# Decays by row transfers, outputs of two steps in token rows, and a new order for all engines

## The chip, the cores and the metric

The kernel runs on one core of a Trainium2 chip. Its engines work side by side, each on its own list of instructions: TensorE (PE, matrix products, with PEld its weight loads), ScalarE (ACT), VectorE (DVE), GpSimd (POOL) and SyncE (SP, which only issues transfers here). Transfers (DMA) are issued by SP, ACT and POOL and carried out by 16 DMA engines. The time is that of one execution on the device, in microseconds (us), as the median of some runs.

## The reference

Two layers, one behind the other. The first is a gated linear attention over 4 batches, 8 heads, 768 tokens and a head size of 48:

```python
f = 1.0 / (1.0 + np.exp(-f_logit))
for t in range(S):
    state = f[:, :, t, :, None] * state + np.einsum('bhd,bhe->bhde', k[:, :, t], v[:, :, t])
    y[:, :, t] = np.einsum('bhd,bhde->bhe', q[:, :, t], state)
```

Its output, as 3072 tokens of 384 values, goes through a gated feed-forward layer with 1536 hidden columns:

```python
gate = np.maximum(x @ w_gate, 0.0)
val = x @ w_val
return (gate * val @ w_out).astype(np.float32)
```

## The kernel before

The 768 tokens are cut into 6 chunks of 128 for each of 4 batches, 24 pieces in all. They are worked off in six steps (c = 0 to 5) of four positions (b = 0 to 3). The eight pieces of steps 0 and 1 are taken as four *units* of two chunks of one batch (function `place`); from step 2 on the step is the chunk and the position is the batch.

An operation is named by letters, step and position (`hq02` is `hq` of step 0, position 2). For one piece:

- `L` load q, k, v and the logits f (`load`, L408 and L413); `ef`, `ln` make -log f (ACT, L484 and L487, for two positions at once).
- `cum` sums the logs over tokens on PE (L505 and L509, later L514). In steps 2 to 4 it also sums each head's columns over the whole chunk, as four matmuls of one column (L517); `dc` makes of these the decay of the state (ACT, L545; L538 in units).
- `ek`, `eq` are the two exponentials (ACT, L528 and L530) into `expo`, `hk`, `hq` the scaled k and q, `hats` (POOL L552 or DVE L553); `v` copies v.
- In steps 0 and 1, `tk`, `tq` transpose them on PE (L564) and `ck`, `cq` copy the result to `qkT`; later `xh` does it by a transposing transfer that SP issues (L572).
- `s` makes the scores (L596, L662), `m` masks them (DVE), `y` (and `yi` in units) multiplies them with v and q with the state, `kv` the update of the state (L784, L707), `ss`, `sd` (L458, L460) the new state with the decay `dec`.
- The output goes to `xT`, with the hidden index on partitions. In steps 0 to 3 (mark `t` of `X_WAY`) `y` is computed turned, as 28 narrow matmuls that write 32 partitions each (L757; L684 and L720 in units), and one copy `x` brings it to `xT`. In steps 4 and 5 (mark `x`), `y` has tokens on partitions, as 4 matmuls of 96 and 8 of 48 columns (L764, L768); `n` copies it to `xn`, and `xx`, a transposing transfer issued by SP (L628), turns it into `xT`.

For each step the feed-forward layer follows: for 12 hidden groups j a gate `g` and a value `u` (three matmuls of 512 tokens each, L804), a relu `r` (L809, L810), a product `p` (L812), then for each position the output `o` in three groups of four matmuls (L825), a copy `d` and a store `S` (L835). The first four hidden groups of step 0 are split into halves of two positions. The weights come as groups by POOL (`wg`, `wv`, `wo`, L435); `wv4+4` is hidden groups 4 to 7.

The order of each engine is written out by hand or by a planner outside of the program, as lists of numbers of operations (`ORDER`). A negative entry stands for filler matmuls on zeros. `BANKS` gives the bank of PSUM for every result in the order of PE. `Plan.link` derives who depends on whom from what is read and written, `lay_out` sets the order, and `waits` makes semaphore waits of it. `HELD` adds waits by hand, mostly for transfers. An engine takes its list strictly in order; so does SP with the transfers that it issues.

Of the kernel before, what the change touches and what calls it, by code (L numbers as in the profile page):

```python
# [6 lines left out]
ALU = mybir.AluOpType  # L7
# [4 lines left out]
NB, NE, NH, NQ, NM, NV, NA, NN, NS, NX, NG, NR, NO = 3, 3, 6, 6, 5, 6, 3, 4, 2, 2, 2, 4, 3  # L12
UNITS = 4
PE_HATS = set(range(0, 8))
X_WAY = "t" * 16 + "x" * 8
# [10 lines left out]
        45, ~60100, 74, 85, ~3512, 82, ~3512, 90, 80, 92, 121, ~1512, 95, 110, 101, 126, ~4512, 116, ~2512, 100, 128,  # L26
# [216 lines left out]
def bass_hgrn2_outer__then__ffn_reglu_kernel(  # L243
# [29 lines left out]
    expo = sb("expo", [128, NE, 2, HD], F32)  # L273
# [681 lines left out]
```

## Time and profile before

| | us |
|---|---|
| median of 3 runs | 193.43 (192.94 to 194.12) |
| the profiled execution | 193.01 |
| its span, first to last instruction | 191.3 |
| PE busy | 180.6 |
| DVE busy | 137.4 |
| ACT busy | 92.0 |
| POOL busy | 59.2 |

The page gives the busy time of each engine, the span in 40 slices (one digit is the busy share in tenths), the transfers, the chain of work that ended last, and the costliest groups of instructions. A row of such a group reads: line, engine, operation, output and inputs, shapes, count, busy time, mean of one in ns, idle time before them and who ended it. A timeline row begins with start and duration in us; its duration is that of the whole row, and matmuls overlap, so that the time that one takes of PE is the distance to the next start.

### The profile page before, as it was taken

What the parts mean: (1) busy time and instruction counts of PE and PEld (TensorE: products, weight loads), DVE (VectorE), ACT (ScalarE), POOL (GpSimd) and SP (SyncE); (2) the same over time, 40 slices, a digit from 0 to 9 for tenths busy, and PEclk for the clock granted to TensorE, in tenths of its full rate; (3) what the DMA queues carried; (4) which work ended last, traced back from release to release, by engine and by line L of the source; (5) the groups of instructions that cost most, each with busy time, mean ns of one, the idle gap of its engine ahead of it and who ended that gap; (6) DMA issues with size and microseconds to landing.
All of it is one profiled execution on the core that took longest, in us unless ns stands there. A gap on an engine that the chain in (4) does not pass through costs nothing.

```text
span 191.3 us, 4793 instructions
## 1 busy us (share of the span) xinstructions
PE 180.6 (94%) x1977; PEld 108.4 (57%) x1996; DVE 137.4 (72%) x249; ACT 92.0 (48%) x200; POOL 59.2 (31%) x88
## 2 busy tenths in 40 slices
PE   7597999989899999999999999999999999999994
PEld 7364785455655556655555654556656554455562
DVE  4299877986758778669868779988688485655620
ACT  3969663264477546497654574372233132301112
POOL 5638531741036702047371610492600000000000
PEclk9999999999999999999999999999999999999999
DMA  6999999969999999989999999999763300000223
GB/s 163 318 296 216 159 209 264 161 123 251 225 221 206 240 201 246 235 191 200 197 182 215 245 175 175 243 251 178 98 151 108 99 4 0 3 0 0 109 98 126
DMA packets 110278, 32.43 MB, mean 170 GB/s; under 512 B 103472, under 2 KB 110000, under 8 KB 110256
## 3 DMA queue, kind: packets, MB, share of 16 engines
q1 hardware_dynamic: 88960, 25.04, 61.7%
q0 software_dynamic: 3744, 3.54, 12.2%
q10 hardware_dynamic: 17552, 3.54, 10.0%
q8 instruction: 16, 0.26, 0.6%
q14 instruction: 6, 0.05, 0.1%
HBM read 25.95 MB, written 4.72 MB: 160 GB/s over the span
## 4 chain that ended last, share of the span: by engine, by line
PE 85%; DVE 8%; DMA 3%; issue 2%; ACT 0%; DVEq 0%; ACTq 0%
PE ps L804 46%; PE ps L825 25%; DVE hats L553 4%; DMA q_in<-in_q_dram 3%; PE ps L596 2%; PE ps L757 2%; PE ps L564 2%; PE ps L514 1%; DVE gT L812 1%; PE ps L662 1%; PE ps L684 1%; PE ps L784 1%; DVE ptm L669 1%; PE ps L768 1%; PE ps L764 1%
## 5 line engine op out<-in xcount | busy, mean ns | idle before, releaser
L812 DVE TENSOR_TENSOR gT<-relu,ps 128x512 bf16<-128x512 bf16 (+1 forms) x76 | 47.7, 653 | 19.7 <-PE ps L804 17.5
L804 PE MATMUL ps<-xT,wv 128*128 128x512 bf16 (+1 forms) x220 | 53.6, 367 | 0.6 <-issue 0.2
L804 PE MATMUL ps<-xT,wg 128*128 128x512 bf16 (+1 forms) x219 | 52.6, 368 | 0.6
L825 PE MATMUL ps<-wo,gT 128*128 128x384 bf16 (+2 forms) x300 | 52.0, 320 | 0.0
L809 ACT ACTIVATE relu<-ps 128x512 bf16<-128x512 f32 (+1 forms) x42 | 23.9, 576 | 47.8 <-PE ps L804 24.2
L825 PEld LDWEIGHTS ps<-wo,gT 128*128 128x128 bf16 x300 | 27.7, 98 | 18.3
L804 PEld LDWEIGHTS ps<-xT,wg 128*128 128x128 bf16 x228 | 23.6, 108 | 20.5 <-issue 0.4
L804 PEld LDWEIGHTS ps<-xT,wv 128*128 128x128 bf16 x228 | 23.3, 108 | 18.3
L552 POOL TENSOR_TENSOR hats<-q_in,expo 128x384 bf16<-128x384 f32 x17 | 17.9, 1058 | 30.2 <-DMA q_in<-in_q_dram 12.2
L810 DVE TENSOR_SCALAR relu<-ps 128x512 bf16<-128x512 f32 (+1 forms) x34 | 21.7, 654 | 5.4 <-PE ps L804 5.3
L552 POOL TENSOR_TENSOR hats<-k_in,expo 128x384 bf16<-128x384 f32 x17 | 17.7, 1050 | 21.2 <-ACT expo L528 14.9
L604 DVE TENSOR_TENSOR ptm<-ps,tri 128x512 bf16<-128x512 f32 x32 | 20.5, 684 | 5.1 <-PE ps L596 5.1
L831 ACT ACTIVATE osb<-ps 128x384 f32<-128x384 f32 (+1 forms) x16 | 7.6, 484 | 25.0 <-PE ps L825 22.2
L528 ACT ACTIVATE expo<-ps 128x384 f32<-128x384 f32 x24 | 11.7, 496 | 6.1 <-DVE hats L553 2.6
L530 ACT ACTIVATE expo<-ps 128x384 f32<-128x384 f32 x24 | 11.8, 492 | 2.0 <-PE ps L517 1.9
L460 POOL TENSOR_TENSOR st<-ssum,dec 128x384 bf16<-128x384 f32 x10 | 8.6, 864 | 10.0 <-DVE ssum L458 10.0
L669 DVE TENSOR_TENSOR ptm<-ps,tmask 128x512 bf16<-128x512 f32 x16 | 10.0, 678 | 2.1 <-PE ps L662 2.1
L484 ACT ACTIVATE f_in<-f_in 128x768 f32<-128x768 f32 x12 | 10.1, 840 | 2.8 <-DMA f_in<-in_f_logit_dram 2.8
L458 DVE TENSOR_TENSOR ssum<-ps,st 128x384 f32<-128x384 f32 x16 | 8.8, 550 | 2.7 <-PE ps L784 2.5
L553 DVE TENSOR_TENSOR hats<-q_in,expo 128x384 bf16<-128x384 f32 x7 | 8.2, 1167 | 3.4 <-DMA q_in<-in_q_dram 3.4
L487 ACT ACTIVATE bneg<-f_in 128x768 bf16<-128x768 f32 x12 | 10.1, 841 | 1.0 <-ACT osb L831 0.8
L564 PE MATMUL ps<-ident,hats 128*128 128x128 bf16 x64 | 5.5, 220 | 4.0 <-DVE hats L553 3.0
(78 smaller groups left out, 159.2 us busy)
## 6 DMA issues: line engine op xcount, KB each, us to landing
v_in<-in_v_dram SPq DMA_DIRECT2D x12, 384.0 KB, 5.5
out_dram<-osb SPq DMA_DIRECT2D x23, 192.0 KB, 2.3
k_in<-in_k_dram SPq DMA_DIRECT2D x10, 384.0 KB, 7.1
q_in<-in_q_dram SPq DMA_DIRECT2D x9, 384.0 KB, 5.8
f_in<-in_f_logit_dram SPq DMA_DIRECT2D x8, 384.0 KB, 4.8
f_in<-in_f_logit_dram ACTq DMA_DIRECT2D x4, 384.0 KB, 6.6
q_in<-in_q_dram ACTq DMA_DIRECT2D x3, 384.0 KB, 5.6
wv<-in_moe_w_val_dram POOLq DMA_DIRECT2D x2, 384.0 KB, 6.7
```

Source lines behind the costliest of these rows:

```text
L484: add(f"ef{c}{b0}", by("ACT", lambda: sc.activation(raw, raw, AF.Exp, scale=-1.0), act_(n)), keys, keys, key=P)
L528: add(f"ek{c}{b}", by("ACT", lambda: sc.activation(ex[:, 1, :], bc.ap[:, 0:HD], AF.Exp, scale=1.0), act_(HD)), [bc], [f"expk{ei}"], key=P + 1)
L530: add(f"eq{c}{b}", by("ACT", lambda: sc.activation(ex[:, 0, :], bc.ap[:, 0:HD], AF.Exp, scale=-1.0), act_(HD)), [bc], [f"expq{ei}"], key=P ...
L552: return {**by("POOL", lambda: gp.tensor_tensor(o, i_, e_, ALU.mult), pool_(HD)), **by("DVE", lambda: ve.tensor_tensor(o, i_, e_, ALU.mult ...
L553: **by("DVE", lambda: ve.tensor_tensor(o, i_, e_, ALU.mult), dve_(HD))}
L604: add(f"m{c}{b}{j}", by("DVE", lambda b=b, j=j, mi=mi: ve.tensor_tensor(ptm[mi][:, j, :, :], s[b, j].ap[:, :].rearrange("p (n t) -> p n t" ...
L669: add(f"m{c}{b2[i]}{j}", by("DVE", lambda i=i, j=j, mask=mask: ve.tensor_tensor(ptm[mi[i]][:, j, :, :], s[j, i].ap[:, :].rearrange("p (n t ...
L804: z = te.matmul(bank.ap[:, 0:n], wt[:, kt, w_cols(j)], xT[xi][:, kt, n0:n1], start=(kt == 0), stop=(kt == NK - 1))
L809: add(f"r{c}{b0}.{j}", {**by("ACT", lambda: sc.activation(rdst, gate.ap[:, 0:n], AF.Relu), act_(n)), **by("DVE", lambda: ve.tensor_scalar_ ...
L810: **by("DVE", lambda: ve.tensor_scalar_max(rdst, gate.ap[:, 0:n], 0.0), dve_(n))}, [gate], [f"relu{ri}"], key=P)
L812: add(f"p{c}{b0}.{j}", by("DVE", lambda: ve.tensor_tensor(gT[gi][:, j, n0:n1], rdst, val.ap[:, 0:n], ALU.mult), dve_(n)), [val, f"relu{ri} ...
L825: z = te.matmul(o.ap[:, 0:e1 - e0], gT[gi][:, j, b * C:(b + 1) * C], wo[:, j, e0:e1], start=(j == 0), stop=(j == NJ - 1))
```

## The change

Four things change.

**Decays as rows.** For the pieces 8 to 19 (steps 2 to 4) the four one-column matmuls in `cum` and `dc` are gone. The last row of `expq`, the exponential at the chunk's last token, holds the same factors. For each pair of positions `xd` fetches it with two small transfers, one for the even and one for the odd heads, from one partition to 48 partitions with 32 bytes each. For that `expo` becomes `expk` (two buffers in place of three) and `expq` (two buffers for pairs, with the head size as the slowest index, so that neighbours in it lie 64 bytes apart). `dec` is laid out anew. A new `eq` into a buffer waits for the `xd` that read it.

**Outputs in token rows.** Steps 2 and 3 get the mark `x` too.

**Smaller constants.** `zeros` has 128 columns, a filler reads them four times; `tlow` shares space with `ssum`. `FOLD`, new in `place` and `load`, has the value of `UNITS`, so that it changes nothing here.

**New orders.** All lists of `ORDER`, `BANKS` and `HELD` are new.

```diff
-NB, NE, NH, NQ, NM, NV, NA, NN, NS, NX, NG, NR, NO = 3, 3, 6, 6, 5, 6, 3, 4, 2, 2, 2, 4, 3
+NB, NE, NH, NQ, NM, NV, NA, NN, NS, NX, NG, NR, NO = 3, 2, 6, 6, 5, 6, 3, 4, 2, 2, 2, 4, 3
+FOLD = 4
+ROW_DECAYS = set(range(8, 20))
+NEQ = 2
-X_WAY = "t" * 16 + "x" * 8
+X_WAY = "t" * 8 + "x" * 16
...
-    expo = sb("expo", [128, NE, 2, HD], F32)
+    expk, expq = sb("expk", [128, NE, HD], F32), sb("expq", [128, NEQ, D, 2, 2, NP], F32)
...
-    decs = sb("dec", [128, NA, B, NP, 2], F32)
+    decs = sb("dec", [128, NA, 2, B, NP], F32)
...
-    tlow = [sb(f"tlow{i}", [128, C], BF16) for i in range(2)]
+    tlow = [ssum[NS - 1][:, C // 2 * i:C // 2 * (i + 1)].bitcast(BF16) for i in range(2)]
-    zeros = sb("zeros", [128, 512], BF16)
+    zeros = sb("zeros", [128, 128], BF16)
...
+        rows = w in ROW_DECAYS
...
             x = te.matmul(bc.ap[:, 0:HD], tri[:, :], bn[:, :, 0:D])
-            if c < NC - 1:
+            if ch < NC - 1 and not rows:
                 for p in range(NP):
                     x = te.matmul(bc.ap[:, HD + p:HD + p + 1], bn[:, 2 * p:2 * p + 2, :].rearrange("p h d -> p (h d)"), ones[:, :])
...
-        ex = expo[:, ei, :, :]
+        ex = (expq[:, eqi, :, :, b % 2, :].rearrange("q d j p -> q p j d"),
+              expk[:, ei, :].rearrange("q (p j d) -> q p j d", p=NP, j=2))
...
+        elif rows and b % 2:
+            b0, c0 = place(c, b - 1)
+            def decay_rows(eng):
+                for j in range(2):
+                    at, to = expq[C - 1:C, eqi, 0, j, 0, 0:1], decs[64 * j:64 * j + D, ai, j, b0, 0:1]
+                    x = eng.dma_start(bass.AP(tensor=to.tensor, offset=to.offset, ap=[list(to.ap[0]), [1, 2 * NP]]),
+                                      bass.AP(tensor=at.tensor, offset=at.offset, ap=[list(at.ap[0]), [4 * NP, D], [1, 2 * NP]]))
+                    if j == 0:
+                        x.then_inc(xd.sem, 16)
+                return x
+            xd = add(f"xd{c}{b - 1}", {**by("SP", lambda: decay_rows(sy), (0.8, 0.8)), **by("ACT", lambda: decay_rows(sc), (0.8, 0.8))},
+                     [f"expq{eqi}_0", f"expq{eqi}_1", f"dec{ai}"], [f"dec{ai}_{b0}", f"dec{ai}_{bt}"], key=P + 2)
+        elif rows:
+            pass
...
         def scaled(src, xh, xe):
-            o, e_ = hats[:, hi, xh, :, 0:D], ex[:, xe, :].rearrange("p (h d) -> p h d", h=H)
-            i_ = src[:, b % 2, :, :]
+            o, e_ = hats[:, hi, xh, :, 0:D].rearrange("q (p j) d -> q p j d", p=NP), ex[xe]
+            i_ = src[:, b % 2, :, :].rearrange("q (p j) d -> q p j d", p=NP)
```

The orders, with the names in place of the numbers, at the places that matter below (F is a filler: count and columns):

```
PE before:   cum00 cum01 [3 F512] tq00 [3 F512] tk01 tk00 tq01 cum03 [F512] s00 cum02 kv00 tk03 [4 F512] tk02 [2 F512] y00 tq03 tq02
             yi01 kv02 s02 g00.3 cum12 g00.2 cum10 u00.3 u00.2 g00.1 y02 yi03 ...
PE after:    cum01 cum00 [2 F512] cum03 cum02 tk01 [2 F512] tk00 [2 F512] tq01 tq00 [F512] tk02 s00 kv00 [2 F512] tq02 [2 F512] tq03 tk03
             y00 yi01 s02 cum10 g00.3 cum12 g00.2 kv02 cum11 y02 yi03 u00.1 ... g00.4 g00.5 tk11 tk10 cum13 ...
ACT after:   ef00 ln00 ef02 ln02 ek01 ek00 eq01 dc00 ek03 eq02 eq00 ek02 ck00 eq03 v01 dc02 ck02 Lq1.0 Lq1.2 ef12 cq02 ef10 ln10 x01
             ln12 eq10 v02 ek10 dc10 eq11 ... r00.6 ek12 eq13 ...
POOL after:  ... hk00 hq01 hk02 v00 hq02 hq03 mtri wv0+2 wg0+2 wv2+2 sd10 v03 wv4+4 wg4+4 hq11 ... hk11 ...
SP before:   Lf0.0 Lf0.2 Lk0.0 Lv0.0 Lk0.2 Lv0.2 Lq0.2 Lf1.2 Lf1.0 Lq1.2 Lq1.0 Lk1.0 Lk1.2 Lv1.2 Lv1.0 ...   (Lq0.0 from ACT)
SP after:    Lf0.0 Lf0.2 Lk0.0 Lq0.0 Lk0.2 Lv0.0 Lq0.2 Lf1.2 Lf1.0 Lv0.2 Lk1.0 Lk1.2 Lv1.0 ...   (Lf1.0 held for wg2+2, Lk1.0 for wv4+4)
PE after, end of step 2:  ... y23 o13.0 cum33 y21 cum30 o12.8 y20 o13.4 o11.0 cum32 kv23 o11.4 o13.8 cum40 o11.8 u20.1 g20.3 ...
PE after, end of step 3:  ... y30 o21.0 o21.4 cum42 y31 o21.8 o20.0 o20.4 o20.8 kv32 o22.8 o23.8 g30.1 ...
SP after, step 2:         ... xh21 xh20 Lf4.0 Lk3.0 S03 xx22 S01 xx23 xx21 xx20 S10 Lv3.0 ...
```

By engine, DVE takes 19 of the 48 `hk` and `hq` (14 before), 11 of the 16 `sd` that can go to either engine (6 before), and 29 of the 76 relus (34 before).

More of the change, by code (lines that the diff above doesn't have):

```diff
@@ L332, in select @@
         add("s" + name, by("POOL", lambda: gp.affine_select(out=ap, in_=ap, **kw), (0.24, 0.29)), [name], [name], key=key)
-    fill("DVE", "zeros", zeros[:], 0.0, 256, -30)
+    fill("DVE", "zeros", zeros[:], 0.0, 64, -30)
     fill("POOL", "tri", tri[:], 1.0, 128, -12 if UNITS else -20)
@@ L352, in bass_hgrn2_outer__then__ffn_reglu_kernel @@
                                                                            channel_multiplier=-2), (0.24, 0.29)), [f"tlow{i}a", f"tlow{i}b"], [f"tlow{i}"], key=-16)
-            add(f"al{i}", by("DVE", lambda low=low, i=i: ve.tensor_tensor(tmask[i][:], tmask[i][:], low[:], ALU.add), (0.12, 0.2)), [f"tlow{i}", f"tmask{i}"], [f"tmask{i}"], key=-15)
+            add(f"al{i}", by("DVE", lambda low=low, i=i: ve.tensor_tensor(tmask[i][:], tmask[i][:], low[:], ALU.add), (0.12, 0.2)), [f"tlow{i}", f"tmask{i}", f"ssum{NS - 1}"], [f"tmask{i}"], key=-15)
         fill("DVE", "pair", pair[:], 0.0, 2, -17)
@@ L398, in place @@
         u = 2 * g + pos // 2
-        return (u % B, u // B * 2 + pos % 2) if u < UNITS else (pos, g)
+        return (u % B, u // B * 2 + pos % 2) if u < FOLD else (pos, g)
     def load(item):
@@ L410, in load @@
             return dma(op, f"{n}{slot}_0", "SP", 64, 0.0193)
-        src = bass.AP(tensor=srcs[n].tensor, offset=b0 * H * S * D + c * C * D, ap=[[D, C], [S * D, (b1 - b0) * H], [1, D]])
-        dst = ld[n][:, slot_of(n, c, b0 // 2), b0 % 2:b0 % 2 + b1 - b0, :, 0:D].rearrange("p b h d -> p (b h) d")
+        dst = ld[n][:, slot_of(n, c, b0 // 2), b0 % 2:b0 % 2 + b1 - b0, :, 0:D]
+        bt, ch = place(c, b0)
+        if 2 * c + b0 // 2 < FOLD:
+            src = bass.AP(tensor=srcs[n].tensor, offset=bt * H * S * D + ch * C * D, ap=[[D, C], [C * D, b1 - b0], [S * D, H], [1, D]])
+        else:
+            src = bass.AP(tensor=srcs[n].tensor, offset=bt * H * S * D + ch * C * D, ap=[[D, C], [S * D, (b1 - b0) * H], [1, D]])
+            dst = dst.rearrange("p b h d -> p (b h) d")
         op = add("L" + item, {**by("SP", lambda: sy.dma_start(dst, src), (0.42, 0.42)), **by("ACT", lambda: sc.dma_start(dst, src), (0.5, 0.5))}, [], in_keys(n, c, b0, b1), key=c * 40 + b0 * 10 - 20 + 0.1 * len(slots))
@@ L450, in new_state @@
         t4 = lambda t: t[:, 0:HD].rearrange("p (n j e) -> p n j e", n=NP, j=2)
-        rate = dec[ai][:, b, :, :].unsqueeze(3).to_broadcast([128, NP, 2, D])
+        rate = dec[ai][:, :, b, :].rearrange("q j p -> q p j").unsqueeze(3).to_broadcast([128, NP, 2, D])
         dk = [f"dec{ai}_{b}", f"dec{ai}"]
@@ L470, in front @@
         w = c * B + b
-        two, cc, bt = w < 2 * UNITS, w // 2 // B * 2, w // 2 % B
+        two, (bt, ch) = w < 2 * UNITS, place(c, b)
+        cc = ch - b % 2
         P = w * 10
         bi, bj = (w // 2) % NB, w % 2
-        ei, hi, qi, ai = w % NE, w % NH, w % NQ, c % NA
+        ei, eqi, hi, qi, ai = w % NE, w // 2 % NEQ, w % NH, w % NQ, ch % NA
         fin, kin, qin, vins = (halves(n, slot_of(n, c, b // 2)) if two else ld[n][:, slot_of(n, c, b // 2), :, :, 0:D] for n in "fkqv")
@@ L523, in front @@
         else:
-            add(f"cum{c}{b}", pe(cum, mm(HD) + (mm(1) * 4 if c < NC - 1 else 0)), ["tri", "ones", f"bneg{bi}", f"bn{bi}_{bj}"], [bc],
+            add(f"cum{c}{b}", pe(cum, mm(HD) + (mm(1) * 4 if ch < NC - 1 and not rows else 0)), ["tri", "ones", f"bneg{bi}", f"bn{bi}_{bj}"], [bc],
                 key=P, opens=[bc])
-        ex = expo[:, ei, :, :]
-        add(f"ek{c}{b}", by("ACT", lambda: sc.activation(ex[:, 1, :], bc.ap[:, 0:HD], AF.Exp, scale=1.0), act_(HD)), [bc],
+        ex = (expq[:, eqi, :, :, b % 2, :].rearrange("q d j p -> q p j d"),
+              expk[:, ei, :].rearrange("q (p j d) -> q p j d", p=NP, j=2))
+        parts = lambda t: t.rearrange("q (p j d) -> q p j d", p=NP, j=2)
+        add(f"ek{c}{b}", by("ACT", lambda: sc.activation(ex[1], parts(bc.ap[:, 0:HD]), AF.Exp, scale=1.0), act_(HD)), [bc],
             [f"expk{ei}"], key=P + 1)
-        add(f"eq{c}{b}", by("ACT", lambda: sc.activation(ex[:, 0, :], bc.ap[:, 0:HD], AF.Exp, scale=-1.0), act_(HD)), [bc],
-            [f"expq{ei}"], key=P + 1)
+        add(f"eq{c}{b}", by("ACT", lambda: sc.activation(ex[0], parts(bc.ap[:, 0:HD]), AF.Exp, scale=-1.0), act_(HD)), [bc],
+            [f"expq{eqi}_{b % 2}"], key=P + 1)
         if two and bj == 0:
@@ L541, in front @@
             add(f"dc{c}{b}", by("ACT", decay2, (0.24, 0.35)), [bc, f"dec{a0}", f"dec{a0 + 1}"], [f"dec{a0}_{bt}", f"dec{a0 + 1}_{bt}"], key=P + 2)
-        elif c < NC - 1 and not two:
+        elif rows and b % 2:
+            b0, c0 = place(c, b - 1)
+            assert c0 == ch and bt == b0 + 1
+            def decay_rows(eng):
[8 more added lines that the diff above has]
+                     [f"expq{eqi}_0", f"expq{eqi}_1", f"dec{ai}"], [f"dec{ai}_{b0}", f"dec{ai}_{bt}"], key=P + 2)
+            dma(xd, f"dec{ai}_{b0}", "SP", 6, 0.013)
+            slots[f"dec{ai}_{b0}"][1] += 16
+            xd.goal += 16
+        elif rows:
+            pass
+        elif ch < NC - 1 and not two:
             def decay():
                 for j in range(2):
-                    x = sc.activation(dec[ai][64 * j:64 * j + 64, b, :, j], bc.ap[64 * j:64 * j + 64, HD:HD + NP], AF.Exp, scale=-1.0)
+                    x = sc.activation(dec[ai][64 * j:64 * j + 64, j, bt, :], bc.ap[64 * j:64 * j + 64, HD:HD + NP], AF.Exp, scale=-1.0)
                 return x
-            add(f"dc{c}{b}", by("ACT", decay, (0.23, 0.34)), [bc, f"dec{ai}"], [f"dec{ai}_{b}"], key=P + 2)
+            add(f"dc{c}{b}", by("ACT", decay, (0.23, 0.34)), [bc, f"dec{ai}"], [f"dec{ai}_{bt}"], key=P + 2)
         def scaled(src, xh, xe):
-            o, e_ = hats[:, hi, xh, :, 0:D], ex[:, xe, :].rearrange("p (h d) -> p h d", h=H)
-            i_ = src[:, b % 2, :, :]
+            o, e_ = hats[:, hi, xh, :, 0:D].rearrange("q (p j) d -> q p j d", p=NP), ex[xe]
+            i_ = src[:, b % 2, :, :].rearrange("q (p j) d -> q p j d", p=NP)
             return {**by("POOL", lambda: gp.tensor_tensor(o, i_, e_, ALU.mult), pool_(HD)),
@@ L554, in front @@
         add(f"hk{c}{b}", scaled(kin, 1, 1), in_k("k") + [f"expk{ei}", f"hats{hi}"], [hk_(hi)], key=P + 2)
-        add(f"hq{c}{b}", scaled(qin, 0, 0), in_k("q") + [f"expq{ei}", f"hats{hi}"], [hq_(hi)], key=P + 2)
+        add(f"hq{c}{b}", scaled(qin, 0, 0), in_k("q") + [f"expq{eqi}_{b % 2}", f"hats{hi}"], [hq_(hi)], key=P + 2)
         if w in PE_HATS:
@@ L736, in back @@
         P = w * 10
+        bt, ch = place(c, b)
         hi, qi, mi, vi, xi = w % NH, w % NQ, w % NM, w % NV, c % NX
@@ L739, in back @@
         y = Bank("a")
-        s_old = st[b][(c + 1) % 2]
-        s_key = [f"S{b}_{(c + 1) % 2}"] if c else []
+        s_old = st[bt][(ch + 1) % 2]
+        s_key = [f"S{bt}_{(ch + 1) % 2}"] if ch else []
         def tiled():
@@ L745, in tiled @@
             rounds = []
-            if c:
+            if ch:
                 for r in range(NK):
@@ L761, in natural @@
         def natural():
-            if c:
+            if ch:
                 for p in range(NP):
@@ L768, in natural @@
                 z = te.matmul(y.ap[:, h * D:(h + 1) * D], ptm[mi][:, h % 2, h // 2, :], vp[:, at:at + D],
-                              start=(c == 0 and h == 0), stop=True, skip_group_check=True)
+                              start=(ch == 0 and h == 0), stop=True, skip_group_check=True)
             return z
@@ L773, in back @@
         if X_WAY[w] == "t":
-            add(f"y{c}{b}", pe(tiled, (7 if c else 4) * mm(C), "c"), need + [f"vpad{vi}"], [y], key=P + 7, opens=[y])
+            add(f"y{c}{b}", pe(tiled, (7 if ch else 4) * mm(C), "c"), need + [f"vpad{vi}"], [y], key=P + 7, opens=[y])
             out_way(c, b, y)
         else:
-            add(f"y{c}{b}", pe(natural, (mm(96) * 4 if c else 0) + mm(D) * 8), need, [y], key=P + 7, opens=[y])
+            add(f"y{c}{b}", pe(natural, (mm(96) * 4 if ch else 0) + mm(D) * 8), need, [y], key=P + 7, opens=[y])
             out_way(c, b, y)
-        if c < NC - 1:
+        if ch < NC - 1:
             kv = Bank("a")
@@ L887, in run @@
                     eng.wait_ge(sems[d.eng], d.val)
+                n = fill % 1000
+                row = zeros[:, 0:n] if n <= 128 else zeros[:].unsqueeze(1).to_broadcast([128, n // 128, 128])
                 for _ in range(fill // 1000):
-                    te.matmul((op.opens[0].ap if op.opens else banks[7])[:, 0:fill % 1000], zeros[:, 0:128], zeros[:, 0:fill % 1000],
+                    te.matmul((op.opens[0].ap if op.opens else banks[7])[:, 0:n], zeros[:], row,
                               start=True, stop=True, skip_group_check=True)
```

8 lines of the change are left out of this document (4 added, 4 removed), and 104 rows, old and new, of tables (BANKS, ORDER).

## The prediction

> **What bounds the kernel now.** I read the page first (busy times, slices, chain), then the windows of ten microseconds, then the chain and the timeline at the places where the change works.
>
> ```profile
> span 191.3 us, 4793 instructions
> PE 180.6 (94%) x1977; PEld 108.4 (57%) x1996; DVE 137.4 (72%) x249; ACT 92.0 (48%) x200; POOL 59.2 (31%) x88
> DVE  4299877986758778669868779988688485655620
> DMA  6999999969999999989999999999763300000223
> PE 85%; DVE 8%; DMA 3%; issue 2%; ACT 0%; DVEq 0%; ACTq 0%
> ```
> ```profile
> 30.00:40.00 10.00, 9.78 (x55) 5.10 (x54) 9.96 (x13) 4.03 (x9) 5.71 (x7) 1.00 1.02 196
> 50.00:60.00 10.00, 9.40 (x228) 5.80 (x229) 6.78 (x13) 6.83 (x14) 3.30 (x4) 1.00 1.36 231
> 100.00:110.00 10.00, 10.00 (x166) 6.29 (x168) 7.78 (x14) 4.66 (x11) 4.28 (x6) 1.00 1.29 231
> ```
>
> TensorE bounds it: 94% busy, 85% of the chain. The window rows give, after span and length, the busy time of PE, PEld, DVE, ACT and POOL, then the clock and the DMA share. From 100 to 110 us PE has no gap, from 50 to 60 it lacks 0.6. So a matmul removed behind 53 us is worth its own time, and every new wait there is lost in full. The second resource is the DMA: its slices read 9 until about 130 us, and its share passes 1.
>
> **The sum, part by part.** The profiled execution took 193.01 us: 191.3 of span and 1.7 around it. The median of the three runs, 193.43, lies 0.4 above it. I sum against 193.01.
>
> *(a) Decays of steps 2 to 4 as rows.* It removes four one-column matmuls from each of twelve `cum`, and twelve pairs of small exponentials on ACT; it adds six pairs of small transfers, two pairs issued by SP and four by ACT.
>
> ```profile
> 79.28 0.08 PE ps L517 x4
> 79.36 0.67 PE ps L825 x4
> 80.03 1.68 PE ps L757 x112
> 81.71 0.76 PE ps L825 x4
> 82.70 0.36 PE ps L784 x8
> ```
> ```profile
> 92.67 0.24 PE L517 MATMUL ps<-ones,bneg 128*128 128x1 bf16 x4
> 92.77 0.32 PE L514 MATMUL ps<-bneg,tri 128*128 128x384 bf16 x1
> L545 ACT ACTIVATE dec<-ps 64x4 f32<-64x4 f32 x24 | 4.0, 166 | 1.1 <-PE ps L517 0.9
> ```
>
> Four such matmuls hold PE for 0.08 us in the chain and 0.10 from 92.67 to 92.77; I take 0.09. Twelve times 0.09 is **1.1 us**, all in stages where PE has no gap. The 4.0 us on ACT count as nothing: ACT is 48% busy. The transfers do not exist in before. Their reader is the state product `sd`, and the state is first read by `y` of the next step, some 30 us later (six steps in a span of 191.3), against landings of up to 7 us for loads a hundred times as large (rows under c). That distance hides them. Without it, SP and ACT would each hold behind the issue, and a late landing would hold the `eq` two pairs later, which now waits for the transfer to have read its buffer. Bounds: nothing, and one landing of 7 us on ACT, which PE would feel only in part; I take nothing, since `eq` stands a whole step behind.
>
> *(b) Outputs of steps 2 and 3 in token rows.* Each `y` becomes 12 full matmuls in place of 28 narrow ones.
>
> ```profile
> 147.08 0.33 PE L764 MATMUL ps<-st,qkT 128*128 128x96 bf16 x4
> 147.25 0.36 PE L768 MATMUL ps<-vpad,ptm 128*128 128x48 bf16 x8
> 147.45 0.33 PE L764 MATMUL ps<-st,qkT 128*128 128x96 bf16 x4
> ```
>
> A narrow group of four takes 1.68 us, and the four L825 behind it 0.76 in place of 0.67, so 1.77. A `y` in rows takes 0.37 (147.08 to 147.45), four 1.48. Two groups save 2 x 0.29, **0.6 us**.
>
> In return the way to `xT` is longer: copy, transposing transfer on SP, landing, where before one copy did.
>
> ```profile
> L609 ACT ACTIVATE xn<-ps x8: 484/491/497, 124.4 to 149.7; 128x384 bf16<-128x384 f32 x8
> L628 SPq DMA_TRANSPOSE xT<-xn x8: 1179/1216/2414, 127.0 to 151.4; - x8
> DMA to landing us min/median/max: 2.3/2.4/5.4
> qkT<-hats SPq DMA_TRANSPOSE x16, 3.3
> ```
>
> The first matmul on the new tokens must not come before the fourth landing. In the new PE order, between the last `y` of step 2 and the first hidden matmul stand five output groups of 0.67 (the row at 79.36), two `cum` of 0.16 (92.51 to 92.67 without its columns) and one `kv` of 0.18 (half of 82.70): 3.85 us. In step 3 it is six groups and one `kv`: 4.20 us. The way itself: copy 0.5, then SP is free about 0.6 after the last `y` (the transpose before it was issued 1.2 us ahead), then the landing. With 2.4 that is 3.0, in time. These stages move more DMA than 127 to 151 us did, so I take the 3.3 of the larger transposes: 3.9, which is **0.1 us** late in step 2 and in time in step 3. The bounds are no wait and 5.4, which is a rival below.
>
> *(c) The start.* The first unit is taken in another order, and q of the first unit now comes from SP, in fourth place.
>
> ```profile
> 8.08 1.15 SPq L408 DMA_DIRECT2D q_in<-in_q_dram  x1
> 19.84 0.50 PE L804 MATMUL ps<-xT,wg 128*128 128x256 bf16 x3
> 21.56 0.81 PE L804 MATMUL ps<-xT,wv 128*128 128x256 bf16 x6
> 22.91 0.73 PE L684 MATMUL ps<-ptm,vpad 64*32 64x128 bf16 x64
> ```
> ```profile
> L552 POOL TENSOR_TENSOR hats<-q_in,expo 128x384 bf16<-128x384 f32 x17 | 17.9, 1058 | 30.2 <-DMA q_in<-in_q_dram 12.2
> L484 ACT ACTIVATE f_in<-f_in 128x768 f32<-128x768 f32 x12 | 10.1, 840 | 2.8 <-DMA f_in<-in_f_logit_dram 2.8
> L530 ACT ACTIVATE expo<-ps 128x384 f32<-128x384 f32 x24 | 11.8, 492 | 2.0 <-PE ps L517 1.9
> q_in<-in_q_dram SPq DMA_DIRECT2D x9, 384.0 KB, 5.8
> k_in<-in_k_dram SPq DMA_DIRECT2D x10, 384.0 KB, 7.1
> f_in<-in_f_logit_dram SPq DMA_DIRECT2D x8, 384.0 KB, 4.8
> wg<-in_moe_w_gate_dram POOLq DMA_DIRECT2D x2, 192.0 KB, 5.6
> ```
>
> The seventh load on SP is the same q as before (8.08), so it lands near 8.08 + 5.8 = 13.9. Two products on POOL follow, `hq02` and `hq03`: 16.0. The first `y` now stands behind their transposes, 16.2. On ACT the copy `x01` stands behind `ef10`, `ln10` and their f. That load is held for a weight group (issued near 4, 5.6 to landing), so SP issues it near 11 and it lands 4.8 later, near 15.8; ACT is then with `ef12` and `cq02` until some 16.4, two passes of 0.84 give 18.1, the copy 18.6. So the first gate matmul comes at about 18.7, against 19.84. Then ACT has to do `ln12`, `eq10`, `v02`, `ek10`, `dc10` (0.84 + 3 x 0.49 + 0.35 = 2.7) before `cum11`, behind which the second unit's `y` now stands: 21.4 to 21.5, against 22.91. By then it has done two half tiles of the hidden layer, before had done five; a half tile is 0.34 (from 21.56 on, six matmuls in 0.68), and `cum11`, 0.16, is done earlier. The lead is 1.4 - 1.0 + 0.16, **0.55 us**. It is the least sure term: a load two microseconds later or earlier moves it by as much, so I keep -1 to +2.
>
> From there to the last `y` of step 1 both orders hold the same matmuls.
>
> ```profile
> 20.00:30.00 10.00, 9.83 (x158) 7.43 (x158) 7.22 (x17) 5.75 (x17) 3.55 (x5) 1.00 1.21 207
> 40.00:50.00 10.00, 9.22 (x120) 5.69 (x120) 7.58 (x16) 4.51 (x9) 2.01 (x4) 1.00 0.93 197
> ```
>
> Before's four windows from 20 to 60 lack 0.17 + 0.22 + 0.78 + 0.60, 1.8 us of PE. I let the new order lose as much, for this reason: it asks for the transposed k of step 1 early, after 14 half tiles (4.8), 8 whole ones (5.2) and some 1.6 us more, at 33.1. The load of that k is held until weight group `wv4+4` has landed (near 27, POOL comes to it at 21). With 5 us it is there at 32 and its product at 33, with the 7.1 of the row above at 35.
>
> *(d) The rest.* DVE takes ten more products (`hk`, `hq`, `sd`) and gives up five relus.
>
> ```profile
> L553 DVE TENSOR_TENSOR hats<-q_in,expo 128x384 bf16<-128x384 f32 x7 | 8.2, 1167 | 3.4 <-DMA q_in<-in_q_dram 3.4
> L460 DVE TENSOR_TENSOR st<-ssum,dec 128x384 bf16<-128x384 f32 x6 | 5.3, 881 | 0.0
> L810 DVE TENSOR_SCALAR relu<-ps 128x512 bf16<-128x512 f32 x30 | 20.1, 685 | 5.1 <-PE ps L804 5.1
> ```
>
> That is at most 5 x 1.17 + 5 x 0.88 - 5 x 0.69, 6.8 us on an engine with 54 us idle; its full slices (30 to 40) lie in the stretch just spoken of. Two filler matmuls fewer, the smaller constants and the shared buffer of `tlow` stand in waits of the first 20 us: nothing.
>
> Sum: 193.01 - 1.1 - 0.6 - 0.55 + 0.1 = 190.9; with half of the 0.4 up to the median, **191.1 us**.
>
> **The rivals.**
> 1. *The longer way to `xT` comes late* (slower). Place: the first hidden matmuls of steps 2 and 3. With landings of L, PE waits L + 0.6 - 3.85 and L + 0.6 - 4.20. At 5.4, the longest of before, that is 2.15 + 1.8 = 4.0 us; without the lead of the start 193.01 - 1.7 + 4.0 = 195.3, and about 195.6 by the median. It eats the whole gain from L = 4.55 on. For it: eight more transposes on a queue that issues 1.2 us for each, where a blocked one holds loads behind it, and a DMA share over 1 in 100 to 110. Against it: the median of 2.4, and that before keeps PE full with the same way in steps 4 and 5.
> 2. *The k of step 1 lands late* (given back). With 7.1 us, its product comes at 35 to 36, and DVE and ACT stand too: `expk` has two buffers now, so `ek12` waits for `hk10`. Two to three us more than before's waits: 193.0.
> 3. *The strided buffer slows the q products.* `expq` is read at a step of 64 bytes. Nearest row:
>
> ```profile
> L609 ACT ACTIVATE xT<-ps x9: 483/491/604, 17.1 to 110.7; 128x384 bf16<-128x384 f32 x9
> ```
>
> The copies of steps 0 and 1, which write every second element, need up to 604 ns, the straight ones 483: a quarter more. With that, a q product on POOL takes 1.32 in place of 1.06, `hq02` and `hq03` end 0.5 us later together, and so do the `y` and the weight issues behind them, which carries the delay once into the gates and once into k: 191.1 + 0.5 + 0.5, 192.1. [...]
> 4. *The start keeps what it gains*: the waits up to 53 us shrink by 1.5: 189.4.
>
> **How the numbers follow.** Forecast 0.33 (190.2 to 192.2), late `xT` 0.22 (194.6 to 198), late k 0.20 (192.2 to 196), stride 0.13 (191.4 to 193), better start 0.12 (188.6 to 190.2). The range from 188.8 to 196.0 leaves out the end of the first rival and little else. One per cent of 193.43 is 1.93 us, about what this measurement tells from no change. Under 191.5 lie two thirds of the forecast and the better start, with a little of the stride: 0.37; over 195.4 most of the first rival and a bit of late k: 0.22; the rest, 0.41, within.
>
> **What would show it.** Right: no one-column matmuls from step 2 on; PE busy about 1.7 us less; steps 2 and 3 without narrow matmuls; the first gate matmul near 18.7 and the last `y` of step 1 done half a microsecond earlier; no PE wait over 0.3 us in front of the first hidden matmul of steps 2 and 3. Wrong: PE idle 1 us and more there, with `xT` landings over 4 us; DVE idle on k near 30 to 35 us; q products on POOL at 1.3 us and more.

## The result and the profile after

The changed kernel is slower: 202.13 us in the median of four executions (201.23 to 203.03), against 193.78 for the kernel before on the same chip. The ratio is 1.0419, with a 95% interval from 1.0331 to 1.0507. The forecast was 191.1, with a range up to 196.0. Some executions take over 1.5% longer than the fastest of their kernel, and the ratios, here and below, leave those out. The profiled execution took 201.23 us with a span of 199.5, which is 8.2 more than the 191.3 of before.

The page after (span, busy times, slices of TensorE and of its clock, chain by engine):

```profile
span 199.5 us, 4441 instructions
PE 183.8 (92%) x1818; PEld 107.9 (54%) x1818; DVE 143.3 (72%) x261; ACT 92.6 (46%) x171; POOL 55.3 (28%) x81
PE   7968899999999799599999659999999999999994
PEclk9999999999999999999999957999999999999999
PE 65%; DMA 14%; SPq 7%; DVE 4%; ACT 4%; issue 2%; POOL 2%; DVEq 0%
```

Three things differ from before. The chain has 14% of DMA and 7% of SP's queue, where DMA had 3% and SP's queue did not appear. TensorE's slices dip to 7 (65 to 70 us), to 5 (80 to 85) and to 6 and 5 (110 to 120), where before was full. And the clock, level before, falls to 5 and 7 tenths from 115 to 125 us, at the end of the third dip and behind it. The list of TensorE's waits says for what (sum, times, longest):

```profile
PE ps L838 <- DMA xT<-xn: 6.7, 2, 4.3
PE ps L597 <- POOL hats L585: 1.3, 4, 0.4
PE ps L629 <- DVE gT L846: 1.1, 1, 1.1
```

The two waits on `xT` stand at the two places of the forecast's first rival, ahead of the first hidden matmul of step 2 and of step 3. In the timeline (start, length, instruction, count, idle time before it):

```profile
81.80 0.81 PE L859 MATMUL ps<-wo,gT 128*128 128x384 bf16 x4
85.06 0.82 PE L838 MATMUL ps<-xT,wv 128*128 128x512 bf16 x3 [2.46 <-DMA xT<-xn]
...
111.42 1.46 PE L859 MATMUL ps<-wo,gT 128*128 128x384 bf16 x8
117.17 1.46 PE L838 MATMUL ps<-xT,wg 128*128 128x512 bf16 x3 [4.28 <-DMA xT<-xn]
...
118.75 3.59 PE L838 MATMUL ps<-xT,wg 128*128 128x512 bf16 x9
```

The reader should also look at the lengths behind the second wait. Three matmuls take 1.46 and nine take 3.59, while behind the first wait three take 0.82. The twelve need 5.0 us (117.17 to 122.17). In the run with step 2 alone (below) the same twelve need 2.8, so the wait of 4.28 is followed by 2.2 us of slow matmuls. Together that is 2.5 + 4.3 + 2.2 = 9.0 us, more than the whole loss.

SP's queue shows where the transfers stood (start, time the issue held the queue):

```profile
72.47 1.62 SPq L423 DMA_DIRECT2D k_in<-in_k_dram  x1
74.14 3.31 SPq L869 DMA_DIRECT2D out_dram<-osb  x1
77.49 1.20 SPq L661 DMA_TRANSPOSE xT<-xn  x1
78.74 0.95 SPq L869 DMA_DIRECT2D out_dram<-osb  x1
79.73 3.77 SPq L661 DMA_TRANSPOSE xT<-xn  x3
...
105.22 1.20 SPq L423 DMA_DIRECT2D k_in<-in_k_dram  x1
106.46 4.92 SPq L661 DMA_TRANSPOSE xT<-xn  x2
111.43 0.58 SPq L869 DMA_DIRECT2D out_dram<-osb  x1
112.05 1.30 SPq L661 DMA_TRANSPOSE xT<-xn  x1
```
```profile
82.25 2.77 DMA xT<-xn
112.05 5.07 DMA xT<-xn
DMA to landing us min/median/max: 2.4/4.0/7.1
```

A store held the queue for 3.31 us ahead of the first transfer of step 2. The fourth of that step was issued at 82.25, 3.1 us after its copy was done (78.70 to 79.19 on ACT), and landed 2.77 us later: here the queue alone made it late. In step 3 two transposing transfers held it for 4.92, and the fourth was issued only at 112.05, when its copy had long been done (108.85 to 109.34 on ACT), and took 5.07 more to land. The two landings are from the chain. The median landing is 4.0, against 2.4 before.

What went as forecast: no one-column matmul is left behind step 1, the narrow groups of steps 2 and 3 are gone, and the start gained. The `cum` behind the last `y` of step 1 begins at 52.15 (chain of after) and at 53.34 in the chain of before:

```profile
52.15 0.43 PE ps L526 x2
```
```profile
53.34 0.27 PE ps L514
```

The balance of the two profiles: -1.2 for the start, -1.7 for the matmuls forecast as saved, +9.0 for the late `xT`, +1.1 for the wait on `gT` at 68.8 us, which before did not have. That is +7.2 of the measured +8.2; the last 1.0 is not accounted for.

### The profile page after: what moved, and what is told of

It is laid out like the page before. It is cut to its first block, busy times and chain, and to the rows that moved or that the text cites. A ratio compares the mean times of both kernels' runs of the same rounds, so it can differ in the third digit from the quotient of the medians.

```text
span 199.5 us, 4441 instructions
## 1 busy us (share of the span) xinstructions
PE 183.8 (92%) x1818; PEld 107.9 (54%) x1818; DVE 143.3 (72%) x261; ACT 92.6 (46%) x171; POOL 55.3 (28%) x81
## 4 chain that ended last, share of the span: by engine, by line
PE 65%; DMA 14%; SPq 7%; DVE 4%; ACT 4%; issue 2%; POOL 2%; DVEq 0%
PE ps L838 38%; PE ps L859 18%; DMA out_dram<-osb 4%; DMA xT<-xn 4%; SPq L413 3%; DMA q_in<-in_q_dram 3%; DMA wg<-in_moe_w_gate_dram 3%; SPq L605 2%; DVE gT L846 2%; POOL hats L585 2%; PE ps L629 2%; PE ps L717 1%; SPq L423 1%; ACT expq L544 1%; PE ps L802 1%
## 5 line engine op out<-in xcount | busy, mean ns | idle before, releaser
L838 PE MATMUL ps<-xT,wg 128*128 128x512 bf16 (+1 forms) x228 | 56.5, 379 | 4.7 <-DMA xT<-xn 4.3
L585 POOL TENSOR_TENSOR hats<-q_in,expq 128x384 bf16<-128x384 f32 x15 | 18.2, 1216 | 24.7 <-ACT expq L544 21.8
L585 POOL TENSOR_TENSOR hats<-k_in,expk 128x384 bf16<-128x384 f32 x14 | 15.3, 1093 | 30.6 <-ACT expk L542 27.9
L544 ACT ACTIVATE expq<-ps 128x384 f32<-128x384 f32 x24 | 19.5, 831 | 8.8 <-PE ps L526 6.4
L865 ACT ACTIVATE osb<-ps 128x384 f32<-128x384 f32 (+2 forms) x15 | 7.0, 466 | 19.8 <-PE ps L859 13.1
L615 POOL CAST vpad<-v_in 128x384 bf16<-128x384 f32 x12 | 6.7, 560 | 29.2 <-DMA v_in<-in_v_dram 25.0
L866 DVE COPY osb<-ps 128x384 f32<-128x384 f32 x10 | 5.6, 556 | 10.9 <-DMA out_dram<-osb 5.9
L542 ACT ACTIVATE expk<-ps 128x384 f32<-128x384 f32 x24 | 11.5, 493 | 2.5 <-DVE hats L586 1.5
L586 DVE TENSOR_TENSOR hats<-q_in,expq 128x384 bf16<-128x384 f32 x9 | 8.6, 952 | 4.1 <-ACT expq L544 4.1
L586 DVE TENSOR_TENSOR hats<-k_in,expk 128x384 bf16<-128x384 f32 x10 | 7.5, 752 | 5.3 <-ACT expk L542 5.3
```

Of the source, the lines that this page charges most:

```text
L542: add(f"ek{c}{b}", by("ACT", lambda: sc.activation(ex[1], parts(bc.ap[:, 0:HD]), AF.Exp, scale=1.0), act_(HD)), [bc], [f"expk{ei}"], key=P ...
L544: add(f"eq{c}{b}", by("ACT", lambda: sc.activation(ex[0], parts(bc.ap[:, 0:HD]), AF.Exp, scale=-1.0), act_(HD)), [bc], [f"expq{eqi}_{b % 2 ...
L585: return {**by("POOL", lambda: gp.tensor_tensor(o, i_, e_, ALU.mult), pool_(HD)), **by("DVE", lambda: ve.tensor_tensor(o, i_, e_, ALU.mult ...
L586: **by("DVE", lambda: ve.tensor_tensor(o, i_, e_, ALU.mult), dve_(HD))}
L838: z = te.matmul(bank.ap[:, 0:n], wt[:, kt, w_cols(j)], xT[xi][:, kt, n0:n1], start=(kt == 0), stop=(kt == NK - 1))
```

## The experiments

Ratios are against the kernel before on the same chip. Executions of the kernels with the new orders scatter by 2 to 7 us, those of before by 2 to 4. A median is over all executions of its run.

| run | what it has | median us | ratio, 95% interval |
|---|---|---|---|
| after | everything | 202.1 | 1.042 [1.033, 1.051] |
| e_turned | steps 2, 3 turned again | 197.8 | 1.013 [1.005, 1.021] |
| e_orders | and decays by matmuls | 198.7 | 1.018 [1.013, 1.022] |
| e_flat | and consecutive `expq` | 198.4 | 1.023 [1.016, 1.029] |
| e_x2 | token rows in step 2 alone | 195.8 | 1.015 [1.010, 1.019] |
| e_x3 | token rows in step 3 alone | 198.5 | 1.025 [1.018, 1.033] |
| e_x2flat | e_x2, matmul decays, consecutive `expq` | 197.5 | 1.011 [1.001, 1.021] |
| e_light | after, 14 loads cut | 196.3 | 1.012 [1.007, 1.017] |
| e_ahead | after, transposes issued earlier | 209.0 | 1.076 [1.068, 1.084] |
| e_pool | after, four loads issued by POOL | 204.8 | none on record |
| e_filler | after, fillers in step 3's wait | 201.4 | 1.039 [1.033, 1.046] |
| b_flat | orders of before, source of after (three `expk` buffers), consecutive `expq` | 193.2 | 1.002 [0.998, 1.005] |
| b_stride | b_flat with the strided `expq` | 196.2 | 1.017 [1.010, 1.024] |
| b_dec | b_stride with row decays | 198.7 | 1.028 [1.021, 1.034] |

**Token rows taken back.** Steps 2 and 3 come out turned; orders and row decays stay.

```diff
-X_WAY = "t" * 8 + "x" * 16
+X_WAY = "t" * 16 + "x" * 8
```

> The changed kernel with steps 2 and 3 back on narrow, turned outputs and one copy to xT; orders and row decays stay. Theory A (the transposing way to xT came late and cost the time): the waits of 2.6 and 4.4 us in front of the first hidden matmuls of steps 2 and 3 go, and with the second the slow clock behind it (about 2.2 us); 0.6 us of narrow matmuls come back: 202.1 - 9.2 + 0.6 = 193.5. Rival B (strided exponentials, the load on the DMA or the orders themselves cost it): the wait only turns up elsewhere, 198 to 201.

197.8 us, ratio 1.013. The ratios differ by 2.9%, some 5.6 us, so the token rows are the larger half of the loss. But 1.3%, 2.5 us, stays without them, and the time lies between the two expectations.

**Decays by matmuls as well.**

```diff
-ROW_DECAYS = set(range(8, 20))
+ROW_DECAYS = set()
```

> As e_turned, and the decays of steps 2 to 4 by one-column matmuls and small exponentials again; what is left of the change are the orders, the strided buffer and the smaller constants. Theory A: the matmuls come back where PE has no gap, 1.1 us over e_turned: 194.6. Rival: the row transfers cost as much as the matmuls did, or the matmuls fall into waits: within 0.4 of e_turned.

198.7 us. By the ratios (1.018 and 1.013) taking the row decays away costs 0.5%, 0.9 us, near the 1.1 forecast, but the intervals overlap: neither the sign nor the size is shown. The loss that stays is in the orders or in the layout of `expq`.

**One step at a time.** The narrow way is put back for step 3 alone (e_x2), and for step 2 alone (e_x3).

```diff
-X_WAY = "t" * 8 + "x" * 16
+X_WAY = "t" * 8 + "x" * 4 + "t" * 4 + "x" * 8    # e_x2
+X_WAY = "t" * 12 + "x" * 12                      # e_x3
```

> The changed kernel with the outputs of step 3 turned again by narrow matmuls, so that only step 2 comes in token rows. Its profile lost 4.45 us on the late xT of step 3 and some 2.2 us on the slow matmuls behind that wait, against 2.6 us on the late xT of step 2. If these waits are the loss, 6 us go and some 0.6 us of narrow matmuls come back: 195 to 197. If the waits only move (the queue is late anyway), 199 or more.

> The other half: step 2 turned again by narrow matmuls, step 3 in token rows. By the waits of the changed kernel's profile 2.6 us go and 0.6 come back: 199 to 200.5. If step 3's transfers were late only because step 2's had delayed the queue, more goes: 196 to 198.

195.8 and 198.5. Against both steps turned (1.013), step 2 alone adds 0.2%, step 3 alone 1.3%, both together 2.9%. So both together seem to cost more than their sum, though by hardly more than the intervals allow. The first time is within its expectation; the second lies between the two values of its own, so how far the transfers of step 2 delay those of step 3 stays open. In the profile of step 3 alone the wait is there, but shorter, and the matmuls behind it keep their pace:

```profile
114.37 0.82 PE L838 MATMUL ps<-xT,wg 128*128 128x512 bf16 x3 [3.32 <-DMA xT<-xn]
115.20 2.10 PE L838 MATMUL ps<-xT,wg 128*128 128x512 bf16 x9
```

Step 2 alone still waits 1.91 us ahead of its first hidden matmul, at 84.32. The chain there goes by an operation on DVE behind a store of 5.01 us that holds an output buffer; but the fourth transfer of `xT`, issued at 81.58 and 2.7 us to its landing, arrives at the same moment, so the late `xT` explains this wait as well. The windows of this run keep a clock of 1.00.

**Is it the order on SP's queue?** The transposing transfers are issued ahead of the stores and loads in front of them.

```diff
-SP: ... Lf4.0 Lk3.0 S03 xx22 S01 xx23 xx21 xx20 ...   Lq4.0 xx32 Lv4.0 Lk4.0 xx33 xx30 S13 xx31 ...
+SP: ... Lf4.0 xx22 xx23 xx21 xx20 S03 S01 Lk3.0 ...   Lq4.0 xx32 xx33 xx30 xx31 Lv4.0 Lk4.0 S13 ...
```

> The changed kernel with the transposes of step 2 issued by SP ahead of two stores and the load of k of step 3, and those of step 3 ahead of the loads of v and k of step 4 and of a store. Theory A1 (the transposes stand behind loads and stores in SP's queue): both waits shrink by half or more, and the clock stays up in step 3: 195 to 197. Rival A2 (the DMA engines are simply full, and a transpose lands late wherever it is issued): the waits stay, 200 to 202.

209.0 us. The waits on `xT` fell to 0.8 us together, as meant, and TensorE waits for what now stands behind them:

```profile
PE ps L838 <- ACT osb L865: 5.0, 1, 5.0
PE ps L838 <- ACT expq L544: 2.7, 1, 2.7
```
```profile
121.74 0.49 ACT L865 ACTIVATE osb<-ps 128x384 f32<-128x384 f32 x1 [9.40 <-DMA out_dram<-osb]
```

ACT stood 9.4 us for an output buffer whose store was queued behind the four transposes:

```profile
103.81 9.30 SPq L661 DMA_TRANSPOSE xT<-xn  x4
116.50 2.24 SPq L869 DMA_DIRECT2D out_dram<-osb  x1
```

The four issues stretch over 9.30 us, though three took 3.77 in step 2 of after, because SP now stands still until each copy is done, with loads and stores behind it. So neither expectation came out: the waits on `xT` shrank, and the time rose beyond both. This order moves the wait; whether one between the two would do without it was not tried.

**Or the issuing engine?** Four of the loads go to POOL.

```diff
-SP:   ... Lf4.0 Lk3.0 ... Lv4.0 Lk4.0 ...
+POOL: ... hq20 Lk3.0 Lf4.0 ... hq31 Lv4.0 Lk4.0 ...
```

> The changed kernel with four loads taken off SP's queue and issued by POOL (decay inputs of step 4, k of steps 3 and 4, v of step 4), the orders otherwise the same. If SP's in-order queue holds the transposing transfers up, the waits on xT ahead of steps 2 and 3 (2.5 and 4.4 us) shrink by half or more and the time is 196 to 199. If the DMA engines themselves are full and the landing is late whoever issues, the waits stay and the time stays at 201 to 202.

Inconclusive. The four executions lie between 199.62 and 206.86 (median 204.8), from just above the first expectation to beyond the second.

**Or full DMA engines?** Fourteen loads of steps 3 and 4 fetch one head of sixteen (a load holds two positions of eight heads; the "twelve" of the expectation is a slip); the issues stay. This leaves that part of the fetching out, and the heads not fetched keep older numbers.

```diff
+            if 2 * c + b0 // 2 >= max(NL[n], 6) and c <= 4:
+                src = bass.AP(tensor=srcs[n].tensor, offset=bt * H * S * D + ch * C * D, ap=[[D, C], [S * D, 1], [1, D]])
+                dst = dst[:, 0:1, :]
```

> The changed kernel with 14 of the loads of steps 3 and 4 (f, k, q, v) cut to the first head of the twelve, the other heads keeping older numbers: it leaves that part of the fetching out, and the number of issues stays. If the transposing transfers are late because the DMA engines are full of these loads, the waits on xT ahead of steps 2 and 3 fall below 1 us together and the time to 193 to 197. If it is the number of issues on SP's queue that holds them, the waits stay at 5 us or more and the time at 199 or more.

196.3 us, 3% less than after, and in its ratio level with e_turned (1.012 and 1.013). In the profiled execution, the fastest of ten with 193.52, one wait on `xT` is left:

```profile
PE ps L841 <- DMA xT<-xn: 2.3, 1, 2.3
```
```profile
106.47 4.97 DMA xT<-xn
```

The wait of step 2 is gone and the issues of the load and the store ahead of its transfers are shorter (0.43 and 1.28 us, in after 1.62 and 3.31), so what the loads move is most of the cause, more than the number of issues; the waits fell to 2.3 us, not below the 1 us that the expectation asked for. The run does not tell the fuller DMA from the earlier landing of the cut loads themselves. Step 3's wait is halved, not gone: its fourth transfer still needs 4.97 us to land (the chain). That transfer stands right behind a store on the queue in after (5.07), in the run with step 3 alone (5.33) and here. That the store makes it slow is not shown: the longest landing of after, 7.1 us, is that of the second transfer of step 3, which stands behind a load.

**The slow matmuls.** Twenty fillers of 512 columns ahead of the first gate matmul of step 3, which compute nothing that is used.

```diff
-PE: ... g30.1 ...
+PE: ... [20 F512] g30.1 ...
```

> The changed kernel with 20 filler matmuls of 512 columns in front of the first gate of step 3, 4.3 us that lie in the wait for xT of 4.4 us. If the low clock from 117 to 122 us comes from the idle time before it, the twelve matmuls there run at full speed: 2.2 us less, 199.9. Rival: the clock falls for another reason, or the fillers only add: 202 to 203.

```profile
114.38 4.48 PE L926 MATMUL ps<-zeros 128*128 128x512 bf16 x20
119.07 0.82 PE L839 MATMUL ps<-xT,wg 128*128 128x512 bf16 x3 [0.21 <-DMA xT<-xn]
119.90 2.10 PE L839 MATMUL ps<-xT,wg 128*128 128x512 bf16 x9
```

At this place the gate matmuls are back at full pace, so their lower pace in after follows from the idle time and not from the operands. The total does not show it: 201.4 us lies between the two expectations, 0.7 from after, which is within the scatter. In the profiled execution (202.52) step 2 waited 3.31 us and its matmuls were slow in turn.

**The layout of `expq`.** In the orders of before, with its decays and turned outputs, the source of after is run with `expq` strided and consecutive. Both runs keep the three buffers of `expk` that before has.

```diff
-expq = sb("expq", [128, NEQ, D, 2, 2, NP], F32)     # b_stride, e_orders
+expq = sb("expq", [128, NEQ, 2, HD], F32)           # b_flat, e_flat
```

> The orders of the kernel before, with its decays and its turned outputs; only the layout of the exp for q is that of the changed kernel (64 bytes from one element to the next). It adds 0.34 us to each eq on ACT and about a quarter of a us to each q product, some 8 us on ACT and 4 on DVE, POOL and the rest. If that is hidden, the time is 193 to 194.5, and the loss that is left in the earlier runs belongs to the orders. If the layout costs on the path, 196 or more.

> The control of the run with the strided layout in the orders of before: the same kernel with the exp for q in consecutive words. If the layout alone made that run slower (196.2 against 193.6), this one is 193 to 194.5. If it is something else of the changed source (fewer buffers for the exp, one scratch tile shared), it stays at 195.5 to 196.5.

196.2 and 193.2: the layout alone costs 3.0 us (1.5% by the ratios), and the rest of the changed source nothing that can be measured. The cut of `expk` to two buffers, which after and all runs with the new orders have, is not in this and was tested nowhere. The groups by tile, strided and then consecutive (min, median and max in ns):

```profile
L542 ACT ACTIVATE expq<-ps x24: 804/825/865, 6.9 to 129.1; 128x384 f32<-128x384 f32 x24
L583 POOL TENSOR_TENSOR hats<-q_in,expq x17: 1183/1194/1639, 16.1 to 139.2; 128x384 bf16<-128x384 f32 x17
L584 DVE TENSOR_TENSOR hats<-q_in,expq x7: 806/1275/2601, 7.9 to 136.1; 128x384 bf16<-128x384 f32 x7
```
```profile
L542 ACT ACTIVATE expq<-ps x24: 475/491/522, 6.9 to 127.0; 128x384 f32<-128x384 f32 x24
L583 POOL TENSOR_TENSOR hats<-q_in,expq x17: 997/1002/1320, 16.1 to 138.3; 128x384 bf16<-128x384 f32 x17
L584 DVE TENSOR_TENSOR hats<-q_in,expq x7: 550/891/2169, 8.5 to 134.3; 128x384 bf16<-128x384 f32 x7
```

The write on ACT is 68% longer, the product on POOL 19%, the shortest on DVE 47%. What in the step of 64 bytes costs this time, and why it differs by engine, is not shown.

> The new orders alone: token rows and row decays are both taken back, and the exp for q is written to consecutive words again instead of 64 bytes apart, so that ACT's eq should take 0.49 us instead of 0.83 and DVE's q products 0.56 instead of 0.82. If the strided layout is what costs, it is 2 to 3 us faster than the same orders with the strided layout (198.7): 195.5 to 196.7. If the orders cost by themselves, it stays at 198 to 199.

198.4 us: with the new orders the consecutive layout brings nothing that can be seen. In the profiled execution a load of the decay inputs landed 9.27 us after its issue, and the whole start came late: the first `cum` of the later steps began at 55.8 us, against 52.15 in after.

```profile
10.54 9.27 DMA f_in<-in_f_logit_dram
```

> The orders of the changed kernel with step 2 in token rows and step 3 turned, the decays computed by one-column matmuls again and the exp for q in consecutive words: the run with step 2 alone (195.8) without the strided layout. If the layout costs here what it costs in the orders of before (3.0 us) and the decays' matmuls come back at 0.9, it is 193 to 194.5, level with the kernel before, and the orders cost nothing by themselves. If the orders cost something by themselves, 196 to 198.5, as the run with both steps turned and the consecutive layout (198.4).

197.5 us, ratio 1.011 with an interval from 1.001 to 1.021: the median lies in the second expectation, the ratio between the two, and that is no answer. The best of these kernels is level with before at most; none beats it.

**Row decays in the orders of before**, the fetch issued by ACT behind the later `eq` of each pair.

```diff
-ACT: ... eq20 ek20 dc22 eq22 ek22 dc23 dc20 ... ek23 eq23 ...
+ACT: ... xd20 (behind eq20, eq21) ... xd22 (behind eq22, eq23) ...
```

> As the run with the strided layout in the orders of before, with the decays of steps 2 to 4 fetched as rows, issued by ACT behind the later eq of each pair. The one-column matmuls go: 48 of them by 0.09 us are 4.3 us of records, of which the prediction counted 1.1 us as path. If that sum is right, 0.5 to 1.2 us less than the run beside it, and 192.5 to 193.5 if the layout is hidden. If the fetch comes late (issue 0.6 us, landing 3 to 5 us), DVE or POOL wait at the state update on the decay and it is 1 us or more slower than the run beside it.

198.7, 2.5 us more than the run beside it. (The 4.3 us of the expectation take 0.09 for each matmul; it is the time of four, and the sum is the 1.1 of the prediction.) ACT's timeline shows what the fetch does there:

```profile
57.19 2.10 ACTq L561 DMA_DIRECT2D dec<-expq  x2
59.34 0.84 ACT L496 ACTIVATE bneg<-f_in 128x768 bf16<-128x768 f32 x1 [2.18 <-issue]
```
```profile
PE ps L524 <- ACT bneg L496: 2.4, 1, 2.4
```

The issue of two transfers of 1.5 KB held ACT for 2.10 us, and TensorE waited 2.4 for the operation behind it. No wait of TensorE is put down to the landing; the issue did the harm.

## Why the prediction was wrong

*What bounds it* held: TensorE does, and its new waits, with the slow matmuls behind one of them, make up most of the loss.

*(a) Decays.* The saving looks right by the ratios (0.9 against 1.1), but it is within the scatter. In after no wait of TensorE is put down to the fetches, though one of them held SP's queue for 2.45 us. "The 4.0 us on ACT count as nothing" was half the account: the fetch needs ACT or SP to issue it, and in the orders of before that alone cost more than the matmuls.

*(b) The way to `xT`: the step that failed.* It took "SP is free about 0.6 after the last `y`" and a landing of 3.3. In after the queue was not free: issues held it 3.31 and 4.92 us, and the fourth transfer of step 3 was issued 2.7 us after its copy was done. The fourth transfer of step 2 was issued 3.1 us after its copy and landed in 2.77, less than forecast: only the queue was wrong there. In step 3 the landing too was longer, 5.07; the median was 4.0. The cover of 3.85 and 4.20 us was worked out well enough; what it had to cover was read from a calmer stretch (127 to 151 us). The term was +0.1 and measured 9.0 in the profile; by the ratios of e_turned and after it is 5.6 with the narrow matmuls saved, so some 6.2 without them.

*Rival 1* was the right mechanism at the right places, and its price too small: 4.0 us from the longest landing, without the queue ahead of the issue and without the slow matmuls behind the wait (2.2).

*(c) The start* gained 1.2 in the profile of after, where 0.55 was forecast; the first gate matmul came at 19.1 (forecast 18.7). The bound of -1 to +2 was too narrow: e_flat's start, in the same orders, was 3.6 us later than after's and 2.4 later than before's. The 1.1 us at 68.8 on `gT` were in no term.

*Rival 2*, the late k, did not come: after waits nowhere on `hats` for more than 1.0 us. *Rival 3*, the stride, was real and sized wrongly, in the opposite direction for its place: POOL's product takes 1.19 and not 1.32, but the write on ACT, which the prediction did not price at all, goes from 0.49 to 0.83, and DVE's read likewise (the shortest from 0.55 to 0.81). Alone it costs 3.0 us where 1.0 was given. *Rival 4*, the better start, came and was lost again.

*What stays open.* After is 4.2% slower: 2.9% go with the token rows, 1.3% stay with e_turned. The layout costs 1.5% in the orders of before, but the parts do not add up in the new orders: without layout, row decays and token rows they still cost 1.6% to 2.9% (e_flat). How much of that is a start that sometimes comes late, how much the two buffers of `expk`, and how much is elsewhere, is not settled.

## What to carry to other kernels

A transfer put in the place of matmuls is paid for on the queue that issues it: count what stands ahead of it there and how long each issue holds the queue in that very stretch (here a store 3.31 us, and 1.28 with the loads cut), and take the landing from a stretch with the same DMA load (for `xT` 4.0 us in the median of after, 2.6 with the loads cut). When a layout is changed to suit one small transfer, price it on every engine that writes or reads the buffer (here 68% on ACT, 19% on POOL, 47% on DVE). And a wait of TensorE of some four microseconds should be charged with the slow matmuls that can follow it, here 2.2 us.

## What the runs showed of the hardware

The clock fell where TensorE had waited. Two windows of 5 us of after, then the first of them in the run with step 2 alone (PE, PEld, DVE, ACT, POOL busy, clock, DMA share, GB/s):

```profile
115.00:120.00 5.00, 2.83 (x10) 1.19 (x11) 0.72 (x2) 1.90 (x4) 1.47 (x2) 0.50 0.89 190
120.00:125.00 5.00, 5.00 (x27) 2.38 (x26) 3.68 (x7) 1.76 (x4) 1.00 (x1) 0.83 0.58 144
```
```profile
115.00:120.00 5.00, 4.74 (x29) 2.27 (x28) 5.00 (x9) 3.49 (x7) 1.19 (x1) 1.00 1.09 200
```

After a wait of 4.28 us the granted clock was 0.50 and then 0.83 in the mean. Windows of 1 us of after show where it changed:

```profile
114.00:115.00 1.00, 0.00 (x0) 0.00 (x0) 1.00 (x1) 0.00 (x0) 1.00 (x2) 0.95 1.16 295
121.00:122.00 1.00, 1.00 (x5) 0.32 (x4) 1.00 (x2) 0.46 (x1) 0.00 (x0) 0.63 0.96 224
```

Between these two it is 0.50. So it was halved from about 114.9 to 121.7 us, some 6.8 us: it fell 2 us into the wait (112.89 to 117.17) and stayed low for 4.6 us of work, of which half, 2.3 us, is lost. That is the 2.2 us of slow matmuls.

The length of a wait alone does not decide. One of 3.31 us was followed by slow matmuls in e_filler (mean clock of that execution 0.992); one of 3.32 in e_x3 left them at full pace (three in 0.82 us, nine in 2.10). In e_flat the clock fell at the end of a wait of 2.40 us, to 0.66 in the mean from 20 to 25 us:

```profile
21.60 0.82 PE L516 MATMUL ps<-bneg,tsum 128*128 128x384 bf16 x2 [2.40 <-ACT bneg L497]
20.00:25.00 5.00, 3.40 (x34) 2.06 (x36) 1.74 (x3) 4.14 (x9) 2.56 (x4) 0.66 1.09 143
```

The issue of a DMA is not free for its engine: in after one store held SP 3.31 us, and in b_dec two transfers of 1.5 KB held ACT 2.10. With the loads cut (e_light) the same store held SP 1.28. But load is not the whole of it: late in after three transposes held SP 4.85 us, against 3.77 for three in step 2, though the DMA share was 0.03 from 155 to 160 us and 0.32 from 160 to 165, against 1.18 from 79.73 to 83.50.

```profile
158.69 4.85 SPq L661 DMA_TRANSPOSE xT<-xn  x3
```
